# Batch 0's rows 96 to 111 by hardware queues, late table parts on GpSimd, batch 2's casts over more units

## The chip, the cores and the metric

One core of one Trainium2 chip runs the kernel. The metric is the device time of one execution in microseconds (us); shorter is better. The engines are PE (matrix products; PEld is its weight loading), DVE (vector), ACT (scalar), POOL (GpSimd, "Pool" in the text) and SP, which here only issues DMAs.

## The reference

Eight batches of 3072 x 256 numbers go through a two-dimensional Fourier transform, of which the real part is kept; the result goes through a feed-forward layer with three weight matrices and an elementwise maximum.

```
X = np.fft.fft(np.fft.fft(x, axis=1), axis=2).real          # x: (8, 3072, 256)
t = X.reshape(24576, 256)
h = np.maximum(np.maximum(t @ w1, t @ w2), t @ w3)          # (24576, 768)
out = h @ w_out                                             # (24576, 256)
```

## The kernel before

**Mixing.** The 3072 rows of a batch are split as 24 x 128 (`a`, `bb`), the 256 columns as 4 x 64 (`g`, `dl`). A batch lies in SBUF as 96 partitions (`g`, `a`) by 128 `bb` by 64 `dl`. In this text "rows 64 to 95" are values of `bb`; one transfer by `load_rows` brings 24 partitions of one `g`, so a range of rows takes four transfers. The real part needs each row together with its mirror image, so each batch is laid out twice as bfloat16: forwards (`lay_rows`, or the cast at L151) and reversed (`reverse`, `turn_rows`, or L154). Stage s (L492 with the forward layout, L494 with the reversed one, seven pieces) transforms over 24 and ends in `z_all`; stage k (L518, L520, six pieces `k(0)` to `k(5)`) transforms over 128 with a table `tab` of sines and ends in `t`. The transform over the columns is folded into the weights once (`prep_first`, L432, from `d2_bf`, `d3_bf` = w2 - w1, w3 - w1; `prep_second`, L451, L461).

**Feed-forward.** Each batch is worked through in 18 units (3 blocks of 512 columns by 6 slices of the hidden layer). A unit has products L538, L539 and L546, their maximum by ACT (L552) and DVE (L553), and a share of the previous block's output products (L563, L576, L587). For the output, DVE makes `other` (L590), Pool adds it to `even` (L593), DVE adds the sum to the products (`ot`, L613), half of which Pool scatters with an indirect DMA (L616, followed by a memset of `mark`) and half of which SP stores (L626). The output products have two PSUM banks; a bank is free again when its L613 is done.

**Order.** Nothing is scheduled: each engine runs its instructions in the order in which the program emits them. The list `plan` hangs pieces on units; they are emitted at the unit's end. Units are counted here from batch 0's first, so unit 24 is batch 1's seventh. Batch 1's stages s and k are spread over units 11 to 20, batch 2's begin at unit 24.

**Start.** Pool issues software transfers that cast to bfloat16 on the way: rows 0 to 95 in twelve transfers (32 rows each), rows 96 to 111 in four (16 rows each), then w1 (L214). SP and ACT bring rows 112 to 127 as float32 into `xs_a`, SP also the next group's first row (`load_next`, L115). SP then waits for one of the software transfers (`last_part[1]`, the fourteenth) and loads w2 and w3 (`raw_w`, L214), then batch 1 in four chunks of 32 rows (L103 by `load_chunk`, four buffers `xs`). DVE and ACT make the constants and the table and then the two layouts `nat` (by `lay_rows`, L365) and `back` (by `reverse` at L136) of batch 0. PE runs 31 warming products (L709) before the first real one. Pool waits with a memset (L410) for the last of DVE's copies (`laid`), then makes the row numbers (`store_rows`), the second halves of `d2_bf` and `d3_bf` (L186) and issues the load of w_out.

**Table.** `tab` has 13 rows of 128 angles, in three parts: sine, cosine, minus sine. `tab_angles` (L270, L274) makes angles, `tab_sines` (L281 to L285, ACT) the first two parts, `tab_minus` (L289) the third. Rows 0 to 6 are made at the start; rows 7 to 9 and 10 to 12 are "late": their angles by DVE at the start, parts of their sines by ACT in units 0, 2 and 3, their third part by Pool in units 1 and 3, each after a chunk of batch 1's casts. `k(3)` (unit 4) needs rows 7 and 8, `k(4)` (unit 6) rows 9 and 10.

**Batch 2's casts.** Pool casts and reverses all later batches. For batch 2 it does 16 half-chunk pieces (`turn_chunk(2, ch, part)`; parts 0 and 1 are L151, parts 2 and 3 L154), two a unit in units 14 to 21. Later batches have one a unit.

Of the kernel before, what the change touches and what calls it, by code (L numbers as in the profile page):

```python
# [9 lines left out]
FP32 = mybir.dt.float32  # L10
# [23 lines left out]
def kernel(  # L34
# [51 lines left out]
    half_pi = consts.tile([128, 64], FP32, tag="half_pi")  # L86
    w_late = consts.tile([128, 6 * 128], FP32, tag="w_late")
    twice = consts.tile([128, 256], FP32, tag="twice")
    sgn = consts.tile([128, 1], FP32, tag="sgn")
# [8 lines left out]
    def load_rows(engs, dst, b, r0, r1, after=None):  # L98
        lds = []
        xr = x_rows(b)  # L100
        for g in range(4):
            eng = engs[g] if isinstance(engs, tuple) else engs
            ld = eng.dma_start(out=dst[g * 24:(g + 1) * 24], in_=xr[g, :, r0:r1, :])  # L103
            if after is not None:
                tc.add_manual_dep(ld.ins, after.ins.name, AFTER, reason="weights first")
            lds.append(ld)
        return lds
# [92 lines left out]
    xs_a = xs_pool.tile([96, 33 * 64], FP32, name="xs", tag="xs")  # L200
    rows_a = xs_a[:, 0:17 * 64].rearrange("p (bb dl) -> p bb dl", dl=64)
    load_rows((nc.sync, nc.sync, nc.scalar, nc.scalar), rows_a[:, 0:16, :], 0, 112, 128)
    load_next(nc.sync, rows_a[:, 16:17, :], 0)

# [4 lines left out]
    for r0 in (0, 32, 64):  # L209
        load_rows(nc.gpsimd, x0v[:, r0:r0 + 32, :], 0, r0, r0 + 32)  # L210
    last_part = load_rows(nc.gpsimd, x0v[:, 96:112, :], 0, 96, 112)

# [7 lines left out]
    for jh in range(2):  # L220
        for wsrc, wdst in zip((moe_w2, moe_w3), raw_w):
            ld = load_w(nc.sync, wdst, wsrc, jh)
            if jh == 0:
                tc.add_manual_dep(ld.ins, last_part[1].ins.name, AFTER, reason="x first")

# [24 lines left out]
    nc.vector.tensor_scalar(out=p128, in0=pidx, scalar1=1.0 / 128.0, scalar2=None, op0=ALU.mult)  # L250
    pi13 = gen.tile([128, 13], FP32, tag="pi13")
    nc.vector.tensor_scalar(out=pi13, in0=j128[:, 0:13], scalar1=pidx, scalar2=1.0 / 3072.0,
                            op0=ALU.mult, op1=ALU.mult)

    step = gen.tile([128, 128], FP32, tag="step")
    near = gen.tile([128, 128], FP32, tag="near")
# [9 lines left out]

    def tab_angles(r0, r1):
        wr = rows_of(r0, r1)
        n = r1 - r0
        nc.vector.tensor_tensor(  # L270
            out=wr.rearrange("p (r j) -> p r j", j=128),
            in0=pi13[:, r0:r1].unsqueeze(2).to_broadcast([128, n, 128]),
            in1=step.unsqueeze(1).to_broadcast([128, n, 128]), op=ALU.subtract)
        nc.vector.scalar_tensor_tensor(out=wr, in0=wr, scalar=0.5, in1=wr,  # L274
                                       op0=ALU.is_gt, op1=ALU.subtract)

# [87 lines left out]
    def lay_rows(copy, xs, r0, n, d0=0, d1=33):  # L364
        return copy(  # L365
            out=xn0[:, d0:d1, r0:r0 + n],
            in_=bass.AP(xs.tensor, xs.offset + d0, [xs.ap[0], [1, d1 - d0], [64, n]]))

    def bf_rows(r0, n):
        return x0_first[:, r0 * 64:(r0 + n) * 64]  # L370

    on_act, on_dve = nc.scalar.copy, nc.vector.tensor_copy
    lay_rows(on_act, xs_a, 112, 16)
    reverse(on_dve, xr0, xs_a, 112, 17)
    on_dve(out=xr0[:, 32, 17:18], in_=xs_a[:, 0:1])
    turn_rows(on_act, 0, 31, 32, 65)
    tab_angles(7, 10)
    tab_angles(10, 13)
    vm = gen.tile([128, 256], FP32, tag="vm")
    qm = gen.tile([128, 256], FP32, tag="qm")  # L380
    nc.vector.tensor_scalar(out=vm[:, 0:128], in0=dvec, scalar1=pidx, scalar2=64.0,
                            op0=ALU.mult, op1=ALU.add)
    lay_rows(on_act, bf_rows(0, 32), 0, 32)
    tab_sines(7, 10, (0, 1))
    turn_rows(on_dve, 31, 32, 32, 65)
    lay_rows(on_dve, bf_rows(32, 32), 32, 32)
    nc.vector.tensor_scalar(out=vm[:, 128:256], in0=dvec, scalar1=pidx, scalar2=None,
# [5 lines left out]
                                   op0=ALU.add, op1=ALU.subtract)  # L393

    nc.scalar.activation(out=md[0], in_=vm, func=AX.Sin, scale=float(-2.0 * math.pi / 256.0))
    for (copy, a, b, c, d) in ((on_act, 54, 65, 20, 33), (on_dve, 32, 54, 0, 20)):
        turn_rows(copy, 63, 32, a, b)
        lay_rows(copy, bf_rows(64, 32), 64, 32, c, d)
    for (copy, a, b, c, d) in ((on_act, 58, 64, 22, 33), (on_dve, 32, 58, 0, 22)):
        turn_rows(copy, 95, 17, a, b)  # L400
        if copy is on_act:
            turn_rows(copy, 95, 16, 64, 65)
        laid = lay_rows(copy, bf_rows(96, 16), 96, 16, c, d)
    nc.vector.tensor_scalar(out=sgn, in0=pidx, scalar1=0.0, scalar2=None, op0=ALU.is_equal)
# [3 lines left out]
    for ch in range(4):  # L408
# [6 lines left out]
    nc.gpsimd.memset(gw[0:1, 512:513], 1.0)  # L415
    store_rows()
    differences(nc.gpsimd, 1)
    nc.gpsimd.dma_start(out=wout_bf.rearrange("p (jc c) -> p jc c", jc=NJC),
                        in_=moe_w_out.rearrange("(jc p) c -> p jc c", jc=NJC))

    def wide(t, cs):
# [362 lines left out]
    for (u, fn) in ((0, prep_some), (0, prep_some), (0, lambda: tab_sines(7, 10, (2,))),  # L784
                    (1, prep_some), (1, prep_some), (1, prep_some),
                    (2, lambda: m.k(2)), (2, prep_some), (2, lambda: tab_sines(10, 13, (0,))),
                    (3, prep_some), (3, lambda: tab_sines(10, 13, (1, 2))),
                    (4, lambda: m.k(3)), (4, prep_some), (5, prep_some), (5, l2_first),
                    (6, lambda: m.k(4)), (7, lambda: m.k(5)), (7, m.end),
                    (0, lambda: turn_chunk(1, 0)), (1, lambda: tab_minus(7, 10, nc.gpsimd)),  # L790
                    (2, lambda: turn_chunk(1, 1)), (3, lambda: tab_minus(10, 13, nc.gpsimd)),
                    (5, lambda: turn_chunk(1, 2)),
                    (7, lambda: turn_last(0)), (8, lambda: turn_last(1)),
                    (8, lambda: lay_last(0)), (9, lambda: lay_last(1)), (20, signed)):
        at(0, u, fn)
    for ch in range(4):
        at(0, (6, 7, 9, 11)[ch], lambda ch=ch: fetch(2, ch))
    for b in range(B - 1):
        for i, whats in enumerate(ahead):
            for what in whats:  # L800
                at(b, begin[b] + i if b else first_ahead[i], lambda b=b, what=what: piece(b + 1, what))
        if b + 2 < B:
            for ch in range(4):
                for part in range(4):
                    at(b, 6 + 4 * ch + part if b else 14 + 2 * ch + part // 2,
                       lambda b=b, ch=ch, part=part: turn_chunk(b + 2, ch, part))
                if b + 3 < B:
                    at(b, UNITS + (0, 1, 2, 4)[ch], lambda b=b, ch=ch: fetch(b + 3, ch))

# [78 lines left out]
```

## Time and profile before

| | us |
|---|---|
| median of 3 runs | 416.05 |
| lowest, highest | 415.71, 417.94 |
| the profiled execution | 416.61 |
| its span in the profile | 414.8 |
| PE busy | 394.1 (95%) |
| DVE busy | 309.2 (75%) |
| ACT busy | 266.9 (64%) |
| POOL busy | 318.2 (77%) |

The span runs from the first to the last instruction that the profile shows; 1.8 us of the execution lie around it. All rows of the profile are of this one execution, whose granted PE clock was 1.0. A row of the timeline gives start, duration, engine, line, operation, output and inputs, shapes and, in brackets, the idle time of the engine before it with what ended it. "xN" at its end means that N instructions in a row are merged. DMA issues appear on the issuing engine (SPq, ACTq, POOL); the duration is that of the issue, not of the transfer.

### The profile page before, as it was taken

How to read it: one execution, taken by the hardware profiler on the slowest of the kernel's cores; microseconds unless marked ns; L12 is line 12 of the kernel's file. 1: busy time of each engine (PE TensorE's matmuls, PEld its weight loads, DVE VectorE, ACT ScalarE, POOL GpSimd, SP SyncE). 2: the span in 40 equal slices, each digit the busy share in tenths (PEclk: the TensorE clock that was granted, in tenths of full speed). 3: DMA queues.
4: the chain of work that ended last, by engine and by line, in shares of the span. 5: the costliest groups of instructions: out<-in, count | busy, mean ns of one | idle time of the engine just before them, and what ended most of it. 6: DMA issues, size and time to landing. Idle time of an engine off the chain costs nothing.

```text
span 414.8 us, 9054 instructions
## 1 busy us (share of the span) xinstructions
PE 394.1 (95%) x3018; PEld 268.4 (65%) x3072; DVE 309.2 (75%) x559; ACT 266.9 (64%) x491; POOL 318.2 (77%) x429
## 2 busy tenths in 40 slices
PE   0988899989999999999999999999999999999996
PEld 0455667756676677667666666666676677766665
DVE  8887676776777777787668767687678777778884
ACT  7877667656765666756775666666676666655550
POOL 9846977999998888888878788888878844545651
PEclk9999999999999999999999999999999999999999
DMA  9998896574317852398216843287412222111314
GB/s 113 141 217 161 173 224 164 154 192 108 123 67 186 195 140 74 96 216 168 97 64 162 205 107 110 88 206 171 133 52 76 66 66 76 66 65 46 110 64 141
DMA packets 131175, 52.70 MB, mean 127 GB/s; under 512 B 113073, under 2 KB 128184, under 8 KB 131128
## 3 DMA queue, kind: packets, MB, share of 16 engines
q1 hardware_dynamic: 106496, 37.50, 36.6%
q0 software_dynamic: 23696, 14.29, 15.5%
q8 instruction: 24, 0.39, 0.4%
q10 hardware_dynamic: 936, 0.33, 0.3%
q14 instruction: 23, 0.19, 0.2%
HBM read 29.02 MB, written 25.17 MB: 131 GB/s over the span
## 4 chain that ended last, share of the span: by engine, by line
PE 86%; SPq 5%; POOL 4%; DMA 2%; issue 1%; DVE 0%; POOLq 0%
PE po L563 29%; PE pse L538 15%; PE pse L546 14%; PE pse L539 12%; SPq L103 4%; POOL x L103 3%; PE po L587 3%; PE ps L518 2%; PE ps L494 2%; PE ps L520 2%; PE ps L492 2%; PE pl L576 2%; DMA xs<-in_x_dram 1%; DMA x<-in_x_dram 1%; SPq L214 1%
## 5 line engine op out<-in xcount | busy, mean ns | idle before, releaser
L552 ACT ACTIVATE stmp<-pse 128x512 bf16<-128x512 f32 x288 | 171.2, 600 | 45.1 <-PE pse L539 26.7
L553 DVE TENSOR_TENSOR hp<-pse,stmp 128x512 bf16<-128x512 f32 x144 | 99.5, 691 | 89.4 <-ACT stmp L552 59.1
L616 POOL DMA_INDIRECT out_dram<-ot,rows_m x92 | 102.5, 1114 | 53.8 <-DVE ot L613 40.8
L538 PE MATMUL pse<-t,gE 128*128 128x512 bf16 x288 | 109.3, 379 | 2.1
L553 DVE TENSOR_TENSOR hm<-pse,stmp 128x512 bf16<-128x512 f32 x144 | 99.1, 689 | 3.7 <-ACT stmp L552 3.5
L539 PE MATMUL pse<-t,gO 128*128 128x512 bf16 x249 | 94.3, 379 | 0.0
L563 PE MATMUL po<-wout_bf,hp 128*128 128x256 bf16 x576 | 85.9, 273 | 0.0
L563 PE MATMUL po<-wout_bf,hm 128*128 128x256 bf16 x570 | 85.3, 273 | 0.1
L593 POOL TENSOR_TENSOR even<-even,other 128x256 f32<-128x256 f32 x92 | 66.5, 723 | 22.7 <-DVE other L590 20.4
L546 PE MATMUL pse<-t,gD 128*128 128x512 bf16 x273 | 82.4, 379 | 0.7
L563 PEld LDWEIGHTS <-hp 128*128 128x128 bf16 x576 | 56.2, 98 | 18.0 <-issue 2.8
L563 PEld LDWEIGHTS <-hm 128*128 128x128 bf16 x576 | 56.3, 98 | 16.6
L613 DVE TENSOR_TENSOR ot<-po,even 128x512 f32<-128x512 f32 x92 | 62.7, 682 | 0.7 <-POOL even L593 0.7
L151 POOL CAST x<-xs 96x544 bf16<-96x544 f32 (+2 forms) x51 | 58.7, 1155 | 4.6 <-DMA xs<-in_x_dram 4.6
L154 POOL CAST x<-xs 96x544 bf16<-96x544 f32 (+5 forms) x57 | 60.5, 1070 | 0.0
L522 ACT CAST t<-ps 128x512 bf16<-128x512 f32 x48 | 27.9, 585 | 36.5 <-PE ps L520 35.3
L546 PEld LDWEIGHTS <-gD 128*128 128x128 bf16 x288 | 27.9, 98 | 32.2
L499 ACT CAST z_all<-ps 128x480 bf16<-128x480 f32 x46 | 25.4, 559 | 35.2 <-PE ps L494 34.2
L590 DVE SCALAR_TENSOR_TENSOR other<-twice,po 128x256 f32<-128x256 f32 x92 | 43.8, 476 | 0.1
L539 PEld LDWEIGHTS <-gO 128*128 128x128 bf16 x288 | 28.1, 98 | 20.0 <-issue 1.8
L538 PEld LDWEIGHTS <-gE 128*128 128x128 bf16 x288 | 28.1, 98 | 19.9 <-issue 0.7
L579 ACT COPY even<-pl 128x512 f32<-128x512 f32 x46 | 27.0, 587 | 9.6 <-PE pl L576 9.2
(168 smaller groups left out, 382.9 us busy)
## 6 DMA issues: line engine op xcount, KB each, us to landing
xs<-in_x_dram SPq DMA_DIRECT2D x84, 198.0 KB
out_dram<-ot SPq DMA_DIRECT2D x90, 128.0 KB
xs<-in_x_dram SPq DMA_DIRECT2D x28, 192.0 KB
raw_w<-in_moe_w_dram SPq DMA_DIRECT2D x4, 384.0 KB
out_dram<-ot,rows_m POOLq DMA_INDIRECT x92, 3.8
x<-in_x_dram POOLq DMA_DIRECT2D x12, 96.0 KB, 5.3
out_dram<-ot SPq DMA_DIRECT2D x17, 64.0 KB
xs<-in_x_dram SPq DMA_DIRECT2D x32, 5.8 KB
```

The costliest lines, as they stand in the source:

```text
L151: nc.gpsimd.tensor_copy(v[:, d0:d1, ch * 32:ch * 32 + 32], xs[:, 0:32 * 64].rearrange("p (bb dl) -> p dl bb", dl=64)[:, d0:d1, :])
L154: reverse(lambda out, in_: nc.gpsimd.tensor_copy(out, in_), v[:, 33:66, :], xs, ch * 32, 33 if ch == 3 else 32, 32 + d0, 32 + d1)
L538: nc.tensor.matmul(pse[:, 0:n], gE[i][:, js], te, start=True, stop=False)
L539: nc.tensor.matmul(pse[:, 0:n], gO[i][:, js], to, start=False, stop=True)
L546: nc.tensor.matmul(pse, gD[i][:, js], to, start=False, stop=True, skip_group_check=True)
L552: nc.scalar.activation(out=stmp[:, 0:n], in_=pses[0][:, 0:n], func=AX.Relu)
L553: nc.vector.tensor_tensor(out=dst, in0=src3, in1=stmp[:, 0:n], op=ALU.max)
L563: nc.tensor.matmul(po, hcols(jc), wout_bf[:, jc * 256:(jc + 1) * 256], start=False, stop=(jc == NJC - 1), skip_group_check=True)
L590: nc.vector.scalar_tensor_tensor(out=other, in0=twice, scalar=po[:, 256:257], in1=po[:, 0:256], op0=ALU.mult, op1=ALU.subtract)
L593: nc.gpsimd.tensor_tensor(out=line[:, 256:512], in0=line[:, 0:256], in1=other, op=ALU.add)
L613: nc.vector.tensor_tensor(out=ot, in0=po, in1=lin, op=ALU.add)
L616: stored(nc.gpsimd.indirect_dma_start(out, bass.IndirectOffsetOnAxis(ap=rows_m[0:128 - lo, b * 12 + slot: b * 12 + slot + 1], axis=0), ot[ ...
```

## The change

Rows 96 to 111 of batch 0 no longer come by four software transfers: SP loads them as float32 into `xs_a` with four transfers behind its first ones. Pool issues twelve transfers of 32 rows, and `raw_w` waits for the ninth of them (the first of rows 64 to 95). DVE and ACT share the layouts anew: the 32 rows 96 to 127 come from `xs_a`; DVE lays rows 0 to 31 out forwards, the two engines share rows 32 to 63, and the last step, shared too, is rows 64 to 95.

Of the late table, the angles of rows 10 to 12 are made by Pool after the issue of w_out's load, in three operations in place of DVE's two; the third part of rows 7 to 9 is made by Pool before the differences, that of rows 10 to 12 in unit 2 ahead of chunk 1's casts.

Batch 2's sixteen half-chunk casts are hung on units 11 to 23, at most two on a unit: 11 11 12 13 14 15 15 16 17 18 19 19 20 21 22 23. The fetch of batch 3's last chunk moves by two units. On PE the order of instructions stays the same.

```diff
     xs_a = xs_pool.tile([96, 33 * 64], FP32, name="xs", tag="xs")
-    rows_a = xs_a[:, 0:17 * 64].rearrange("p (bb dl) -> p bb dl", dl=64)
-    load_rows((nc.sync, nc.sync, nc.scalar, nc.scalar), rows_a[:, 0:16, :], 0, 112, 128)
-    load_next(nc.sync, rows_a[:, 16:17, :], 0)
+    rows_a = xs_a.rearrange("p (bb dl) -> p bb dl", dl=64)
+    load_rows((nc.sync, nc.sync, nc.scalar, nc.scalar), rows_a[:, 16:32, :], 0, 112, 128)
+    load_next(nc.sync, rows_a[:, 32:33, :], 0)
+    load_rows(nc.sync, rows_a[:, 0:16, :], 0, 96, 112)
...
     for r0 in (0, 32, 64):
-        load_rows(nc.gpsimd, x0v[:, r0:r0 + 32, :], 0, r0, r0 + 32)
-    last_part = load_rows(nc.gpsimd, x0v[:, 96:112, :], 0, 96, 112)
+        last_part = load_rows(nc.gpsimd, x0v[:, r0:r0 + 32, :], 0, r0, r0 + 32)
...
             if jh == 0:
-                tc.add_manual_dep(ld.ins, last_part[1].ins.name, AFTER, reason="x first")
+                tc.add_manual_dep(ld.ins, last_part[0].ins.name, AFTER, reason="x first")
...
-    def tab_angles(r0, r1):
+    def tab_angles(r0, r1, eng=nc.vector):
...
+        if eng is nc.vector:
...
+        else:
+            eng.tensor_scalar(out=w_high[:, 0:n * 128], in0=wr, scalar1=0.5, scalar2=None,
+                              op0=ALU.is_gt)
+            eng.tensor_tensor(out=wr, in0=w_high[:, 0:n * 128], in1=wr, op=ALU.subtract)
...
-    lay_rows(on_act, xs_a, 112, 16)
-    reverse(on_dve, xr0, xs_a, 112, 17)
-    on_dve(out=xr0[:, 32, 17:18], in_=xs_a[:, 0:1])
+    lay_rows(on_act, xs_a, 96, 32)
+    reverse(on_dve, xr0, xs_a, 96, 33)
+    on_dve(out=xr0[:, 32, 33:34], in_=xs_a[:, 0:1])
     turn_rows(on_act, 0, 31, 32, 65)
+    lay_rows(on_dve, bf_rows(0, 32), 0, 32)
     tab_angles(7, 10)
-    tab_angles(10, 13)
...
-    lay_rows(on_act, bf_rows(0, 32), 0, 32)
     tab_sines(7, 10, (0, 1))
     turn_rows(on_dve, 31, 32, 32, 65)
-    lay_rows(on_dve, bf_rows(32, 32), 32, 32)
...
+    lay_rows(on_act, bf_rows(32, 32), 32, 32, 17, 33)
     nc.scalar.activation(out=md[0], in_=vm, func=AX.Sin, scale=float(-2.0 * math.pi / 256.0))
-    for (copy, a, b, c, d) in ((on_act, 54, 65, 20, 33), (on_dve, 32, 54, 0, 20)):
-        turn_rows(copy, 63, 32, a, b)
-        lay_rows(copy, bf_rows(64, 32), 64, 32, c, d)
-    for (copy, a, b, c, d) in ((on_act, 58, 64, 22, 33), (on_dve, 32, 58, 0, 22)):
-        turn_rows(copy, 95, 17, a, b)
+    lay_rows(on_dve, bf_rows(32, 32), 32, 32, 0, 17)
+    for (copy, a, b, c, d) in ((on_act, 55, 64, 21, 33), (on_dve, 32, 55, 0, 21)):
+        turn_rows(copy, 63, 33, a, b)
         if copy is on_act:
-            turn_rows(copy, 95, 16, 64, 65)
-        laid = lay_rows(copy, bf_rows(96, 16), 96, 16, c, d)
+            turn_rows(copy, 63, 32, 64, 65)
+        laid = lay_rows(copy, bf_rows(64, 32), 64, 32, c, d)
...
     store_rows()
+    tab_minus(7, 10, nc.gpsimd)
     differences(nc.gpsimd, 1)
     nc.gpsimd.dma_start(out=wout_bf.rearrange("p (jc c) -> p jc c", jc=NJC),
                         in_=moe_w_out.rearrange("(jc p) c -> p jc c", jc=NJC))
+    tab_angles(10, 13, nc.gpsimd)
...
-                    (0, lambda: turn_chunk(1, 0)), (1, lambda: tab_minus(7, 10, nc.gpsimd)),
-                    (2, lambda: turn_chunk(1, 1)), (3, lambda: tab_minus(10, 13, nc.gpsimd)),
+                    (0, lambda: turn_chunk(1, 0)), (2, lambda: tab_minus(10, 13, nc.gpsimd)),
+                    (2, lambda: turn_chunk(1, 1)),
...
-                    at(b, 6 + 4 * ch + part if b else 14 + 2 * ch + part // 2,
+                    at(b, 6 + 4 * ch + part if b else 11 + 13 * (4 * ch + part) // 16,
...
-                    at(b, UNITS + (0, 1, 2, 4)[ch], lambda b=b, ch=ch: fetch(b + 3, ch))
+                    at(b, UNITS + (0, 1, 2, 4 if b else 6)[ch], lambda b=b, ch=ch: fetch(b + 3, ch))
```

More of the change, by code (lines that the diff above doesn't have):

```diff
@@ L87 @@
     w_late = consts.tile([128, 6 * 128], FP32, tag="w_late")
+    pi_all = consts.tile([128, 64], FP32, tag="pi_all")
+    pi13 = pi_all[:, 0:13]
+    step = consts.tile([128, 128], FP32, tag="step")
+    w_high = consts.tile([128, 3 * 128], FP32, tag="w_high")
     twice = consts.tile([128, 256], FP32, tag="twice")
@@ L250 @@
     nc.vector.tensor_scalar(out=p128, in0=pidx, scalar1=1.0 / 128.0, scalar2=None, op0=ALU.mult)
-    pi13 = gen.tile([128, 13], FP32, tag="pi13")
     nc.vector.tensor_scalar(out=pi13, in0=j128[:, 0:13], scalar1=pidx, scalar2=1.0 / 3072.0,
                             op0=ALU.mult, op1=ALU.mult)
-    step = gen.tile([128, 128], FP32, tag="step")
     near = gen.tile([128, 128], FP32, tag="near")
@@ L265, in rows_of @@
         return (w_late if r0 >= 7 else w)[:, (r0 % 7) * 128:(r0 % 7 + r1 - r0) * 128]
-    def tab_angles(r0, r1):
+    def tab_angles(r0, r1, eng=nc.vector):
         wr = rows_of(r0, r1)
         n = r1 - r0
-        nc.vector.tensor_tensor(
+        eng.tensor_tensor(
             out=wr.rearrange("p (r j) -> p r j", j=128),
@@ L273, in tab_angles @@
             in1=step.unsqueeze(1).to_broadcast([128, n, 128]), op=ALU.subtract)
-        nc.vector.scalar_tensor_tensor(out=wr, in0=wr, scalar=0.5, in1=wr,
-                                       op0=ALU.is_gt, op1=ALU.subtract)
+        if eng is nc.vector:
+            eng.scalar_tensor_tensor(out=wr, in0=wr, scalar=0.5, in1=wr,
+                                     op0=ALU.is_gt, op1=ALU.subtract)
+        else:
+            eng.tensor_scalar(out=w_high[:, 0:n * 128], in0=wr, scalar1=0.5, scalar2=None,
+                              op0=ALU.is_gt)
+            eng.tensor_tensor(out=wr, in0=w_high[:, 0:n * 128], in1=wr, op=ALU.subtract)
     def tab_sines(r0, r1, parts=(0, 1, 2)):
```

## The prediction

> **What bounds the kernel now.** All times are us from the start of the profiled execution; line numbers are those of the kernel before. First the page: PE is busy 95% of the span, and the chain of work that ended last puts nearly all of it on PE.
>
> ```profile
> PE 86%; SPq 5%; POOL 4%; DMA 2%; issue 1%; DVE 0%; POOLq 0%
> ```
>
> So only PE's idle time can be won or lost. I looked for it in PE's own timeline, keeping the rows with idle time before them.
>
> ```profile
> 18.55 0.20 PE L492 MATMUL ps<-m24f,nat 96*128 96x96 bf16 x1 [0.80 <-DVE sgn L404]
> ...
> 22.09 0.82 PE L432 MATMUL psg<-d_bf,md_all 128*128 128x384 bf16 x4 [0.64 <-DVE d_bf L186]
> ...
> 25.95 0.81 PE L432 MATMUL psg<-d_bf,md_all 128*128 128x384 bf16 x4 [0.37 <-POOL d_bf L186]
> ...
> 35.67 0.27 PE L518 MATMUL ps<-tab,z_all 128*128 128x256 bf16 x1 [0.77 <-POOL tab L289]
> ...
> 43.87 0.27 PE L518 MATMUL ps<-tab,z_all 128*128 128x256 bf16 x1 [1.31 <-POOL tab L289]
> ...
> 91.74 0.27 PE L587 MATMUL po<-gw,t 128*128 128x257 bf16 x1 [0.94 <-DVE ot L613]
> ```
>
> These six are where the change can act; after 100 us the table of 10 us stretches has PE busy 9.89 to 9.95 of 10 up to 410. Next, what feeds the first rows: Pool's timeline, a piece of the chain of waits, and the stretch from 5 to 10 us (busy time and count of PE, PEld, DVE, ACT, POOL; then clock, DMA share, GB/s).
>
> ```profile
> 1.47 13.91 POOL L103 DMA_DIRECT2D x<-in_x_dram  x16 [0.29 <-issue]
> 15.37 1.77 POOL L214 DMA_DIRECT2D w_bf<-in_moe_w_dram  x2
> ...
> 12.53 3.49 DMA x<-in_x_dram
> ...
> 5.00:10.00 5.00, 0.55 (x2) 0.29 (x3) 4.43 (x30) 4.39 (x12) 5.00 (x7) 1.00 2.07 123
> ```
>
> Pool issues 16 software transfers of batch 0's rows until 15.37. The 14th, issued at 12.53, lands at 16.02 and lets SP start raw_w. DVE and ACT then lay the rows out:
>
> ```profile
> 9.23 0.99 DVE L136 CAST back<-xs 96x544 bf16<-96x544 f32 x2
> ...
> 12.26 1.10 DVE L136 COPY back<-x 96x1056 bf16<-96x1056 bf16 x1
> ...
> 17.50 0.53 DVE L136 COPY back<-x 96x442 bf16<-96x442 bf16 x1 [0.58 <-DMA x<-in_x_dram]
> ...
> 9.14 1.10 ACT L365 CAST nat<-xs 96x528 bf16<-96x528 f32 x1
> ```
>
> Both engines work almost without a break from 9.2; DVE waits only 0.58 for the last rows. So the start is set nearly as much by this copying as by the transfers. Last, Pool around the stall at 91.74:
>
> ```profile
> 90.25 0.72 POOL L593 TENSOR_TENSOR even<-even,other 128x256 f32<-128x256 f32 x1
> 90.92 2.32 POOL L154 CAST x<-xs 96x561 bf16<-96x561 f32 x3
> 93.39 0.98 POOL L616 DMA_INDIRECT out_dram<-ot,rows_m  x1 [0.16 <-DVE other L590]
> ```
>
> This L593 had its operand since DVE's L590 at 85.13, five us earlier: two casts a unit in units 14 to 21 have put Pool behind.
>
> **Part 1, rows 96 to 111 by SP.** Pool loses transfers 13 to 16, 15.37 - 11.83 = 3.5 us, though each is half size (0.7 to 1.0 us, against 0.82 to 0.87 for most full ones). SP gains four issues behind its nine, at about 4.5 to 6.2 (0.4 each, by its rows at 0.74 and 1.23); nothing queued behind them was ready, since raw_w waited until 16.02 anyway. When do these rows land? They are 4 x 24 x 16 = 1536 rows. SP's and ACT's first four transfers move as many, issued from 0.74 to 2.0, and their packets end at about 4.5: some 3.8 from the first issue, so 8.3 with nothing beside them. Beside the software stream, whose 10752 rows take about 11.6 us by the packet records (930 a us), they may get half the turns: 1536 / 465 = 3.3 us. With 1.45 from issue to first packet (raw_w: 16.04 to 17.5) and 0.45 from last packet to use (17.0 to 17.46) that is 4.5 + 5.2 = 9.7. I take 10.0. The software rows are held up by 0 (engines not full) to 1536 / 930 = 1.65 us (full); I take 0.7.
>
> The Trainium skill, "DMA: Bandwidth & Descriptors", section "Issuing engines are not separate DMA queues", says that transfers from all issuers share the same 16 engines, so that another issuer saves only issue time. That rule would mean the full 1.65 us, rival B below.
>
> **The copies of the first rows.** The new order on DVE, from the steps of before (start to start): reversing 33 rows in place of 17 from xs, 1.2 in place of 0.67; lay_rows of rows 0 to 31, 1.0; one pair of tab_angles, 1.05 (the other, 1.05, has gone to Pool); vm 0.25; reverse 32 rows 1.0; vm to L392 1.2; half a lay_rows 0.55: 6.3 in all, then 0.75 + 0.75 for rows 64 to 95. ACT: lay 32 rows from xs 2.0 in place of 1.0, reverse 1.9, sines 1.1, half a lay 1.0, md 0.35, then 0.6 + 0.2 + 0.85: 8.0. From 10.0 DVE ends at 17.8 and ACT at 18.0; from 9.15, as before, ACT ends at 17.15, but PE's 31 warming products last until 17.76 in any case. Rows 64 to 95 were in by 15.51 (DVE reversed them then without a wait), so with 0.7 more by 16.2, when both engines get to them. PE starts at about 18.2 in place of 18.55: **0.35 won**, between -0.9 (rows seen at 11.2) and 0.75.
>
> **raw_w, then everything behind it.** SP now waits for the ninth transfer. It was issued at 8.18 and took 5.2 to land: 13.4 in place of 16.02. With the hold-up above the shift is 2.6 down to 1.0; I take 1.9. w1 moves 3.5 earlier on Pool. Then the waits of 0.64 (DVE's raw_w) and 0.37 (Pool's) go, even with PE 0.35 early.
>
> **Part 2, the table on Pool.** tab_minus(7,10), 1.18, now runs at about 19.5 before the differences, where Pool waited 3.59 for raw_w: free, and the 0.77 at 35.67 goes. tab_minus(10,13) moves ahead of chunk 1's casts: it ends near 35.5, the products that waited at 43.87 come near 40, so 1.31 goes. tab_angles(10,13) is new work on Pool, three operations of 128x384: tensor_tensor 128x256 took 0.72 and 128x768 1.65, so about 0.95 twice, and 1.18 for the comparison (L289's): 3.1 after the wout issue, ending near 30.3 (26.37 + 1.65 + 0.92 - 1.9 + 3.1). ACT's sine of these rows ran at 31.63 and wants it near 30.2: 0 to 0.8 of a wait, taken as 0.1. Chunk 0's casts wait for it too, but were waiting for their transfer (to 30.34 - 1.9 = 28.4) and are not what is late next.
>
> What is late next is wout: its products at 36.25 waited for its transfer, whose issue shifts with raw_w, by 1.9. So PE's gain there is the smaller of 0.35 + 0.64 + 0.37 + 0.77 = 2.1 and 1.9. With 1.31 it is **3.2** at unit 6. Batch 1's chunks also land 1.9 earlier, and Pool saves a tab_minus between them (1.18), so its casts, which before ended 0.4 ahead of PE's first use at 56.2, end 3.1 earlier: no new stall.
>
> **Part 3, batch 2's casts over units 11 to 23.** In old time, Pool's idle 2.8 and 1.4 us at 60.5 to 65.8 now take four half-chunk casts, and with one cast in most units the sum (casts 1.1, L593 0.7, L616 with its memset 1.25) keeps up: the L593 that came at 90.25 comes near 86.5, and the stall of 0.94 is gone but for 0.2 or so. But the last cast now stands behind unit 23's L616, which waits for that unit's ot. DVE's L590 there is at 89.80, ot ends at 90.97 at best, L616 runs to 92.15, and the cast (1.2 by L173's two) to 93.45. Adding up Pool's work from 59.8 on, cast by cast, gives 93.8. PE's first reversed product of batch 2 was at 93.11 before, both stalls included; now 93.5 to 93.85. **0.7 lost** (0.3 to 0.9): the stall moves and grows.
>
> The rest costs nothing: pi, step and the scratch tile move to another pool without an instruction, and batch 3's last chunk is fetched two units later, 12 units (over 30 us) ahead of its first cast, on an SP queue that waits for stores there anyway.
>
> **Sum.** 3.2 - 0.7 = 2.5 on the profiled execution, 416.61 (414.8 of span and 1.8 around it): 414.1. The median of the runs is 416.05, 0.56 lower: 413.5.
>
> **Rivals.** *A, all of the gain*: the engines have room, x and raw_w come as early as the rows of before allow (2.6), PE starts at 17.8, the last cast costs 0.3: 0.75 + 0.64 + 0.37 + 0.77 = 2.5, with 1.31 and less 0.3 it is 3.5: 412.5. For it: the DMA share falls with Pool's smaller transfers, so Pool set the pace. *B, the transfers share full engines*: raw_w shifts by 1.0 and PE's start by nothing: 1.0 + 1.31 - 0.8 = 1.5, 414.5. For it: a share of 2.07 that hardly varies at 4 to 11 us. *C, raw_w overtakes x (slower)*: before, two half transfers were open behind the one that releases raw_w, and x was in (17.0) when raw_w's first packets came (17.5); now three full ones, 2304 rows, are open. If many are still open 1.45 us after the release, each turns with a raw_w packet; raw_w's 1.57 MB take 5.5 us at the 283 GB/s of 19 to 20 us. All of that on x (15.4 to 20.9) starts PE at 22.6, 4.05 late; the four removed waits (3.1) and the cast's 0.7 stay: -4.05 + 3.1 - 0.7 = -1.65, 417.7; half of it gives 415. It decides from 3.9 us of delay on; against it, the ninth lands late (5.2), when most later rows have moved. "DMA: Bandwidth & Descriptors" of the Trainium skill, section "Queues, rings and completion order", has each engine take turns between its queues by packets, which is how C would work. *D, no effect at the start*: the copies take longer than I add up and only the Pool table's 1.31 and the casts count: 416.05 - 0.6.
>
> **How the numbers follow.** Forecast 0.51 (its own range 412.8 to 414.4), A 0.14, B 0.15, C 0.12, D 0.04, and 0.04 for a loss that no row of before shows. A measurement of this kernel tells about 0.5%, 2.1 us, from no change, so faster is under 414.0: 0.44 of the forecast and all of A, 0.58. Slower, over 418.1, needs C at its worst with a longer cast stall (0.04) or the unseen loss (0.04): 0.08. The same: 0.34. Range 411.8 to 416.9: it leaves out C's upper end, the unseen loss and a little of A, under 0.2.
>
> **What would show it.** Right: 12 software issues ending near 11.9, raw_w issued at 14 to 15, PE's first L492 near 18.2, no idle before the L518 of 35.67 and 43.87, and a PE wait of 1.4 to 1.8 on Pool's last L154 of batch 2 (near 91) in place of L587's 0.94. Wrong: ACT or DVE idle at 9.2 for over 2 us; x rows landing after 17; a new wait of ACT for w_late; PE waiting for batch 1's casts near 53.

## The result, and the profile after

The changed kernel takes 422.34 us (median of 4 runs, 422.22 to 423.02); the kernel before, run beside it, 415.88. The ratio is 1.0154, interval 1.0111 to 1.0198: slower, and outside the range that was forecast. The profiled execution took 422.26 with a span of 420.5, which is 5.7 longer than before. Line numbers from here on are those of the changed kernel (3 to 7 more than before), unless a version of the kernel before is named.

The page first: the busy line of PE, and the chain that ended last.

```profile
PE 398.1 (95%) x3018; PEld 271.2 (64%) x3072; DVE 308.7 (73%) x556; ACT 266.3 (63%) x489; POOL 318.7 (76%) x428
...
PE 91%; POOL 2%; DVE 2%; issue 2%; DMA 1%; ACT 0%; DVEq 0%; POOLq 0%; ACTq 0%
```

PE does the same instructions, yet is busy 4.0 longer (394.1 before): part of the loss is not waiting at all. In the first 100 us, behind the warming products, PE's timeline has two waits left of over half a microsecond:

```profile
21.39 0.20 PE L497 MATMUL ps<-m24f,nat 96*128 96x96 bf16 x1 [2.28 <-DVE sgn L407]
...
96.61 0.22 PE L499 MATMUL ps<-m24r,x 96*128 96x96 bf16 x1 [3.36 <-POOL x L158]
```

All six rows that the prediction showed are gone or replaced: the waits for `d_bf`, for the two negated table parts and for the bank (L587 before) are away, as forecast. (For the two of the table this is not shown to be the table's doing: in e_rows below, where the table is made as before and PE also comes late, they are gone too.) In their place stand a start 2.84 later (21.39 against 18.55) and a wait of 3.36 for Pool's last cast of batch 2. What feeds the start, in the timeline of ACT, DVE, Pool and SP:

```profile
13.30 2.01 ACT L372 CAST nat<-xs 96x1056 bf16<-96x1056 f32 x1 [4.05 <-DMA xs<-in_x_dram]
...
13.60 1.20 DVE L140 CAST back<-xs 96x1056 bf16<-96x1056 f32 x2 [4.27 <-DMA xs<-in_x_dram]
...
1.47 10.01 POOL L107 DMA_DIRECT2D x<-in_x_dram  x12 [0.29 <-issue]
12.11 0.75 POOL L218 DMA_DIRECT2D w_bf<-in_moe_w_dram  x1 [0.62 <-DMA x<-in_x_dram]
...
15.60 0.42 SPq L218 DMA_DIRECT2D raw_w<-in_moe_w_dram  x1
```

Pool's issues do end early (11.5 instead of 15.4). But rows 96 to 111, on SP's queue since 4.93, are read only at 13.3; ACT and DVE, which the prediction wanted to feed at 10.0, stand idle for over 4 us; and `raw_w` goes out 0.44 earlier than before, not 1.9.

Then the clock. These are stretches around both waits (busy time and count of PE, PEld, DVE, ACT, POOL; granted PE clock; DMA share; GB/s):

```profile
22.00:25.00 3.00, 3.00 (x42) 3.00 (x39) 2.30 (x5) 1.12 (x2) 2.60 (x6) 0.50 0.92 169
...
94.00:97.00 3.00, 0.39 (x9) 0.39 (x10) 0.00 (x0) 0.00 (x0) 3.00 (x5) 1.00 0.14 27
97.00:101.00 4.00, 4.00 (x20) 2.05 (x18) 1.74 (x3) 1.97 (x4) 1.44 (x2) 0.57 0.45 97
```

After each of the two waits PE works at half its clock for 3.41 us, by the clock records of the trace from 21.96 to 25.38 and from 97.06 to 100.47. Half of 3.41, twice, is 3.4 of the 4.0 us of extra busy time. Last, Pool around the second wait:

```profile
90.69 1.18 POOL L158 CAST x<-xs 96x561 bf16<-96x561 f32 x1
91.82 0.72 POOL L598 TENSOR_TENSOR even<-even,other 128x256 f32<-128x256 f32 x1
92.90 2.59 POOL L621 DMA_INDIRECT out_dram<-ot,rows_m  x1 [0.36 <-DVE hp L558]
...
95.52 1.20 POOL L158 CAST x<-xs 96x495 bf16<-96x495 f32 x2
```

The last cast stands behind a scatter that took 2.59. The prediction gave it 1.0, what the others take.

As a ledger: batch 1's first product comes at 57.25 against 56.22 before (+1.0; 3.2 earlier was forecast), the second group of ten of batch 2's first products at 100.97 against 95.78 (+5.2 in all), the end +5.7. The last 0.5 was not taken apart.

### The profile page after: what moved, and what is told of

It reads as the page before. It is cut to its first block, busy times and chain, and to the rows that moved or that the text cites. A ratio compares the mean times of both kernels' runs of the same rounds, so it can differ in the third digit from the quotient of the medians.

```text
span 420.5 us, 9047 instructions
## 1 busy us (share of the span) xinstructions
PE 398.1 (95%) x3018; PEld 271.2 (64%) x3072; DVE 308.7 (73%) x556; ACT 266.3 (63%) x489; POOL 318.7 (76%) x428
## 4 chain that ended last, share of the span: by engine, by line
PE 91%; POOL 2%; DVE 2%; issue 2%; DMA 1%; ACT 0%; DVEq 0%; POOLq 0%; ACTq 0%
PE po L568 30%; PE pse L543 16%; PE pse L551 15%; PE pse L544 13%; PE ps L497 3%; PE ps L499 3%; PE po L592 3%; PE ps L523 3%; PE ps L525 3%; PE pl L581 2%; POOL x L107 2%; DMA x<-in_x_dram 1%; DVE nat L372 1%; DVE hm L558 0%; DVE back L140 0%
```

## The experiments

Theory 1: rows 96 to 111 come late because their packets share the same transfer engines with Pool's software stream. Theory 2: batch 2's stall is the last cast behind the batch's last scatter. Theory 3, formed on seeing the first results: a wait of PE is paid twice, since the clock halves after it. "Before" is each time the median of the kernel before on the same chip. It lay between 414.9 and 416.1, so where a version is called nearer than the changed kernel, its distance from "before" is set against the changed kernel's 6.5.

### The parts alone

**e_rows**: the kernel before with the change at the start only (the first hunks of the diff; `raw_w` behind the ninth transfer).

> Only the rows part (rows 96 to 111 by SP, raw_w behind the ninth transfer, the layouts shared anew); table and casts as before. Theory 1 (the start was lost to the hardware rows, which get a third of the turns beside the software stream): ACT and DVE wait some 4 us at 9.2, the rows are seen at 13.3, PE's first product is at 21.4, its clock then drops for 3 to 4 us, and stage k begins near 26.6, 3.9 later than before. The table waits of 0.77 and 1.31 shrink or vanish, since Pool's casts of batch 1 are no later than before and PE is; at unit 6 some 1.6 remain and nothing gives them back: slower than before by 1.0 to 2.5. Rival (all of 5.7 us was lost at the start and only shows later): slower by 4 or more.

420.82, before 415.37, ratio 1.014 (1.0092 to 1.0188); four runs from 418.74 to 423.0, the profiled one being the lowest. `xs` is read at 13.4 and 13.7, PE starts at 22.50 after 4.32 idle, and 23 to 27 us pass at a clock of 0.50 to 0.76. DVE still makes the angles of rows 10 to 12 here (1.05), which the expected 21.4 left out. Part 1 alone loses 5.4 by the medians, where theory 1 had said 1.0 to 2.5 and its rival 4 or more: the size went to the rival. The profiled execution lost 2.2 of span; why two of the four took 422 to 423 is not shown.

**e_table**: the kernel before with the table's part only.

> Only the table part (angles of rows 10 to 12 by Pool, both third parts earlier on Pool). Theory (as forecast): PE's idle 0.77 and 1.31 go, the first is partly taken by the wait for w_out, so faster by 1.3 to 2.1; the waits at the start (0.80, 0.64, 0.37) and the stall of 0.94 at 91.7 stay. Rival (DVE loses 1.05 of work at the start and Pool gains 3.1): if DVE sets the start, PE also starts up to 0.5 earlier, 2.5; if Pool's 3.1 hold up chunk 0's casts or ACT's sine, no gain.

414.88, ratio 0.9988 (0.9971 to 1.0006): not clear of no change, where 1.3 to 2.1 were expected. The 0.77 and the 1.31 are gone, but there are new waits on PE and, for the late angles, on ACT; the last three lines are Pool's:

```profile
28.58 0.81 PE L440 MATMUL psg<-d_bf,md_all 128*128 128x384 bf16 x4 [0.54 <-POOL d_bf L190]
34.19 0.38 PE L546 MATMUL pse<-t,gE 128*128 128x512 bf16 x1 [0.41 <-ACT stmp L560]
...
32.64 0.52 ACT L288 ACTIVATE tab<-w_late 128x384 bf16<-128x384 f32 x1 [0.46 <-POOL w_late L282]
...
20.84 1.19 POOL L296 TENSOR_SCALAR tab<-tab 128x384 bf16<-128x384 bf16 x1
24.24 1.64 POOL L190 TENSOR_TENSOR d_bf<-raw_w,w_bf 128x768 bf16<-128x768 f32 x1 [2.22 <-DMA raw_w<-in_moe_w_dram]
26.89 1.64 POOL L190 TENSOR_TENSOR d_bf<-raw_w,w_bf 128x768 bf16<-128x768 f32 x1 [1.00 <-DMA raw_w<-in_moe_w_dram]
```

The negation (L296) holds nothing up here: behind it Pool still waits 2.22 and then 1.00 for `raw_w`, and the 0.54 on PE comes from that second wait. e_best2 below, which has no negation at this place, shows the same two waits (0.97 on Pool, 0.51 on PE). ACT's sine does wait for Pool's angles. Up to batch 1's first product 1.4 was won.

**e_casts**: the kernel before with batch 2's casts over units 11 to 23 only.

> Only the casts part (batch 2's casts over units 11 to 23). Theory 2 (the last cast stands behind the scatter of the batch's last slot, which takes 2.6 and not 1.0): that scatter takes 2.6, PE waits 3 to 3.5 at the first reversed product of batch 2, its clock drops for some 4 us behind that wait, and with the 0.94 and 0.28 of before gone the kernel is slower by 3.5 to 4.5. Rival (the forecast's size: scatter 1.0, wait 1.8, no drop of the clock): slower by 0.3 to 0.9.

420.55, ratio 1.0095 (1.0065 to 1.0124); the six times lie in two groups, 418.1 and 418.2, and 420.5 to 420.9. By the medians that is 5.2 slower, more than the 3.5 to 4.5 expected. The scatter and the wait are as theory 2 has them, and its rival falls:

```profile
91.71 2.58 POOL L616 DMA_INDIRECT out_dram<-ot,rows_m  x1 [0.20 <-DVE hp L553]
...
95.41 0.22 PE L494 MATMUL ps<-m24r,x 96*128 96x96 bf16 x1 [3.19 <-POOL x L154]
```

The three parts alone don't add up to the whole: 5.4 - 0.5 + 5.2 is 10.1, against 6.5 for the changed kernel. Where the difference lies was not taken apart.

### The scatter

**e_scatter112**: the changed kernel, with the scatter of each batch's last slot shortened from 127 rows (from partition 1 on) to 112 (from partition 16 on). It leaves 15 rows of every batch but the last unwritten.

```diff
-  ap=rows_m[0:128 - lo, ...], ot[lo:128, 256:512]
+  ap=rows_m[0:128 - 16 * lo, ...], ot[16 * lo:128, 256:512]
```

> The changed kernel, but the scatter of each batch's last slot moves 112 rows instead of 127 (the 15 rows left out are not written in any batch but the last). Theory 2a (127 rows are what makes it slow, since they don't divide over the engines): it takes about 1.0, PE's wait for the last cast falls from 3.4 to about 1.8 and its clock stays up, so faster than the changed kernel by 1.6 to 3.6: 418.7 to 420.7. Rival (it is slow because of its place, at a batch's end, or because it waits for its queue): it stays at 2.6 and the time stays at 422.3.

418.07, ratio 1.0064 (1.0039 to 1.0089): 2.7 over the kernel before, so 3.8 nearer than the changed kernel.

```profile
90.39 0.97 POOL L621 DMA_INDIRECT out_dram<-ot,rows_m  x1 [0.17 <-DVE hp L558]
```

With 112 rows the scatter takes 0.97 like one with 128; with 127 it takes 2.59. Whether the number of rows or the first partition does it stays open, since this version changes both. PE's wait fell to 1.54 and no half clock followed. Its ten times fall in two groups, and the mean granted clock of each run sorts them: five runs at 416.15 to 417.14 have 1.000, five at 419.01 to 419.78 have 0.991 to 0.994. The profiled one is of the first: PE started at 20.64 after 2.60 idle, at full clock. So the same program runs with a half clock in some executions and without it in others, which makes a difference of about 2.6; at which place it came in the other five is not seen, since they have no trace.

**e_after22**: the changed kernel with the sixteen casts over units 11 to 22, so that none follows the batch's last scatter; all the work is done.

```diff
-  11 + 13 * (4 * ch + part) // 16
+  11 + 12 * (4 * ch + part) // 16
```

> The changed kernel with batch 2's casts over units 11 to 22 instead of 11 to 23, so that no cast stands behind the batch's last scatter of 2.59; all the work is done, and the late start is still in. Theory (that scatter is the whole of the loss at batch 2): PE idle under 0.5 at batch 2's first product, no half clock there, time 416.0 to 418.3, as in the run with scatters of 112 rows (418.07). Rival (the casts of the last units come late in any order): over 1.5 idle there, time over 420.

417.16, ratio 1.0036 (1.0005 to 1.0067): 2.0 over the kernel before, so 4.5 nearer than the changed kernel, and PE has no wait of note at batch 2. This is most of the loss, removed by one number. Four of its runs have a clock of 0.992 to 0.996; the fifth, at 1.000, took 414.49.

### The start

**e_warm38**: the changed kernel with 38 warming products (`range(31)` becomes `range(38)`).

> The changed kernel with 38 warming products instead of 31, so that they last about 2.2 us longer (0.31 each), to some 21.3, and PE has next to no idle time ahead of its first transposing product at 21.39 (2.28 in the changed kernel). Theory: the half clock in 22 to 25 comes from that idle time and not from the transposing products; then the granted clock stays at 1.0 in 20 to 28, the last step of the start (stage k) comes at 24.3 to 25.0 instead of 26.63, batch 1's first product 1 to 2.3 earlier than 57.25, and the time falls by 1 to 2.3, to 420 to 421.3. Rival: the clock falls whatever PE did before, since the products themselves or the transfers draw it down: clock 0.5 again, time within 0.5 of 422.3.

420.24, ratio 1.0121 (1.0087 to 1.0155). The changed kernel's is 1.0154, and the two intervals overlap, so what tells here is the trace. PE starts almost when it did, with less idle time ahead; the second line is the stretch after it, with the clock ahead of the last two numbers.

```profile
21.29 0.20 PE L497 MATMUL ps<-m24f,nat 96*128 96x96 bf16 x1 [1.06 <-DVE sgn L407]
...
22.00:25.00 3.00, 2.97 (x59) 2.38 (x55) 2.66 (x6) 2.36 (x7) 2.60 (x6) 1.00 0.86 143
```

59 products instead of 42 in the same 3 us: theory 3 holds for the start, and batch 1's first product came 1.7 earlier (55.59).

**e_early**: the changed kernel with rows 96 to 111 issued ahead of the next row (`load_rows` moved above `load_next`).

> The changed kernel with the four transfers of rows 96 to 111 ahead of SP's five small ones of the next row, so 2.3 earlier in SP's queue; nothing else. Theory 1 (those transfers lose turns to the software stream that begins to move at 4.0, and get some 360 packets of 256 B per us beside it instead of 410 on this queue alone): rows seen at 10.5 to 11.5 instead of 13.3, PE's first transposing product at 18.9 to 19.7 instead of 21.39, so idle under 0.8 and no half clock at the start; batch 1's first product 54.5 to 55.5; time 419.0 to 420.5, with batch 2's late cast still in. Rival (the queue is in order and its 3168 packets take as long however they are ordered, to 13): rows seen at 12.8 to 13.4, time within 0.7 of 422.3.

420.3, ratio 1.0116 (1.0081 to 1.0151). Half right: ACT reads its rows at 10.35, but DVE's reversal also needs the next row, which is now behind them and is seen at 12.74. PE started at 20.70, a microsecond later than expected, after 1.79 idle, and the half clock came again.

**e_spread**: the same, and two of the four transfers by ACT.

```diff
-    load_rows(nc.sync, rows_a[:, 0:16, :], 0, 96, 112)
+    load_rows((nc.sync, nc.sync, nc.scalar, nc.scalar), rows_a[:, 0:16, :], 0, 96, 112)
```

> As the kernel before it in this list (rows 96 to 111 ahead of the next row), and two of the four transfers issued by ACT, whose queue moved 440 packets per us beside SP's 410 in 3 to 4 us; ACT pays 0.97 for the two issues. Theory 1a (each hardware queue has turns of its own): rows seen by 8.5 to 9.9, where ACT and DVE become free, PE's first transposing product at 17.5 to 18.5, no half clock at the start, batch 1's first product 53.0 to 54.5, time 417.5 to 419.5 with batch 2's late cast still in. Rival 1b (the two hardware queues share one third of the turns beside the software stream): rows seen at 10.5 to 11.5, as with one queue, time 419.0 to 420.5.

420.2, ratio 1.0119 (1.0082 to 1.0156).

```profile
9.17 1.96 ACT L372 CAST nat<-xs 96x1056 bf16<-96x1056 f32 x1
...
12.43 1.30 DVE L140 CAST back<-xs 96x1056 bf16<-96x1056 f32 x2 [3.10 <-DMA xs<-in_x_dram]
```

The rows themselves were in time, so theory 1a's arrival was right, but not its 417.5 to 419.5: the next row was late, and PE started at 20.27. Its idle time was 1.63, with no half clock at the start; batch 1 began at 54.75. The next row's last packet moved at 10.66, 1.8 before DVE read it; in the changed kernel that distance is 0.5 (12.80 to 13.30). What fills the rest is not shown.

**e_spread2**: the split between the queues, with the next row back ahead of SP's half.

> The changed kernel with rows 96 to 111 issued half by SP (still behind its five small transfers of the next row) and half by ACT; nothing else. With the rows ahead of the next row, DVE waited for the next row instead (12.43); this order leaves the next row where it was. Theory (two queues, and 768 packets on SP's in place of 1536): both reads of the rows at 9.2 to 10.3, PE's first transposing product at 17.5 to 18.6, no half clock at the start, batch 1's first product 52.5 to 54.5; time 417.5 to 419.3, with batch 2's late cast still in. Rival (the start is held by the software rows and the copies behind them, not by rows 96 to 111): reads at 9.2 to 10.3 but the first transposing product at 19.5 to 20.5, time 419.8 to 420.6.

420.47, ratio 1.0133 (1.0105 to 1.016). A miss: 12.62 for ACT, 12.91 for DVE. SP's 768 packets still had to pass beside the software stream, and ACT's first sine began 2.4 later (5.88 instead of 3.44). In these versions whatever was put last on the queues was read at 12.4 to 13.7.

**e_ready**: rows ahead of the next row and on two queues, DVE's angles and its copy of rows 0 to 31 moved ahead of the reversal into the gap, 29 warming products, casts to unit 22.

> The changed kernel with rows 96 to 111 ahead of the next row and half on ACT's queue (rows at 9.2 for ACT, next row at 12.4 for DVE, as that version showed), DVE doing the table's angles (1.1) and the copy of rows 0 to 31 (1.1) in the gap of 3.1 ahead of its reversal, 29 warming products, and batch 2's casts to unit 22. Theory (the start follows the copies, and these the arrival): PE's first transposing product at 17.8 to 18.8 instead of 20.27 there, batch 1's first product 52.3 to 53.5, no half clock; time 411.0 to 412.8, under every version so far (413.55). Rival (what the shorter stream brings is lost in the waits for the experts' weights behind it): first transposing product at 17.8 to 18.8, but batch 1's first product at 54.0 or later, time 413.3 to 415.

415.48, ratio 0.9987 (0.9969 to 1.0005): no gain, though the waits for `xs` are gone. Neither side was right, since PE started at 19.91. What is late next are the software rows:

```profile
15.54 1.09 ACT L372 COPY nat<-x 96x512 bf16<-96x512 bf16 x1 [0.40 <-DMA x<-in_x_dram]
...
15.57 1.09 DVE L140 COPY back<-x 96x1056 bf16<-96x1056 bf16 x1 [0.79 <-DMA x<-in_x_dram]
```

Both read rows between 31 and 63. In the kernel before DVE began to reverse them at 12.26 and to lay them out at 13.28, without a wait. What the hardware rows gain in time, the software rows lose. (PE's idle time was 2.35, and the half clock came here too.)

**e_norows** tests that. It is e_after22 without the hardware transfers of rows 96 to 111: DVE fills their place with zeros, and the 12 software transfers stay.

> The changed kernel with batch 2's casts to unit 22, and with rows 96 to 111 of batch 0 not loaded at all: DVE fills their place with zeros (some 1.1, behind its table), so the output lacks these rows; the 12 software transfers stay. Theory (the hardware packets took their turns from the software stream): x's 9216 software packets end at 15.0 to 15.6 instead of 16.99 (the kernel before moved 10752 of them in the 13.2 from 3.9 to 17.16, so 11.4 for 9216), PE's first transposing product at 17.3 to 18.6, time 412.5 to 415. Rival (the software stream has a pace of its own, set by Pool's issues or its ring): its packets end at 16.5 to 17.0 again, PE's first transposing product at 18.6 or later, time over 415.

412.34, ratio 0.9923 (0.9902 to 0.9945).

```profile
18.26 0.20 PE L497 MATMUL ps<-m24f,nat 96*128 96x96 bf16 x1 [0.45 <-DVE sgn L407]
...
12.78 2.52 SPq L217 DMA_DIRECT2D raw_w<-in_moe_w_dram  x4
```

Batch 1's first product comes at 52.56. From the packet records of the trace, in us (software packets of 128 B, one for a row of 64 numbers; hardware packets of 256 B):

| kernel | software: count, first, half, last | hardware: count, last |
|---|---|---|
| before | 10752, 3.84, 9.88, 17.08 | 1632, 8.40 |
| changed | 9216, 3.86, 10.96, 16.95 | 3168, 12.80 |
| e_spread | 9216, 4.93, 10.51, 16.39 | 3168, 10.66 |
| e_norows | 9216, 3.96, 9.16, 14.88 | 1632, 8.21 |

Taking 1536 software packets away ends the stream 2.2 earlier (17.08 to 14.88). Putting the same rows back as hardware packets costs 2.1 of that (16.95); over the five traces with the changed kernel's transfers the stream ends between 16.50 and 17.14, so it is 1.6 to 2.3. Theory 1 is shown, and more than that: the rows of x take their turns whichever queue they come by, so the change had next to nothing to win in the arrival of x. Even without these rows PE starts only 0.29 earlier than in the kernel before (18.26 against 18.55); what e_norows wins lies behind that, with `raw_w` issued 3.26 earlier (12.78 against 16.04).

### Versions meant to be faster

**e_casts22**: the kernel before with the casts over units 11 to 22 alone.

> The kernel before with batch 2's casts spread over units 11 to 22 alone. Theory: the stall of 0.9 in unit 23 of batch 0 goes and nothing comes in its place; time 0.3 to 1.0 under the kernel before. Rival (the faster times of the version with the moved table parts came from those alone): within 0.3 of the kernel before, or over it.

414.57, before 415.15, ratio 0.9975 (0.9958 to 0.9993), and the wait of 0.94 is gone: as forecast.

**e_best2**: the same, and the two negations moved, with all angles left on DVE.

```diff
+    tab_minus(7, 10, nc.gpsimd)          # behind the issue of w_out's load
...
-    (0, lambda: turn_chunk(1, 0)), (1, lambda: tab_minus(7, 10, nc.gpsimd)),
-    (2, lambda: turn_chunk(1, 1)), (3, lambda: tab_minus(10, 13, nc.gpsimd)),
+    (0, lambda: turn_chunk(1, 0)), (2, lambda: tab_minus(10, 13, nc.gpsimd)),
+    (2, lambda: turn_chunk(1, 1)),
```

> The kernel before, with two things alone: both negated table parts leave their old place (the first goes on Pool behind the output weights' issue, the second ahead of the second turning of batch 1), the angles stay on DVE; and batch 2's casts are spread over units 11 to 22, so that the last one follows a scatter of 128 rows and not the batch's last one of 127 rows, which takes 2.59. Theory: the waits of 0.77 and 1.31 for the negated parts go, the new waits of the version with angles on Pool (0.54, 0.41, 0.24) don't come, the last cast is done by 93 and PE waits less than 0.3 at batch 2's first product, and the stall of 0.9 in unit 23 of batch 0 goes; time 412.5 to 414.2 against 415.4. Rival: the last cast is still ahead of the batch's last scatter or behind it at PE's need (over 1.5 idle and a lower clock again): 417 to 420.

413.55, before 414.9, ratio 0.9963 (0.9945 to 0.9981), 12 runs from 412.95 to 415.1. Pool around the same place as above, in the lines of this version:

```profile
88.00 1.23 POOL L154 CAST x<-xs 96x495 bf16<-96x495 f32 x2
...
90.12 2.58 POOL L617 DMA_INDIRECT out_dram<-ot,rows_m  x1 [0.20 <-issue]
```

The scatter is as long as ever, but the last cast is ahead of it, and PE has no wait there. Two waits for `d_bf` behind Pool, of 0.52 and 0.51, came all the same. Batch 1 begins at 54.25, 1.7 earlier than in e_casts22 (55.99). Of the versions that do all the work this is the fastest, though its interval overlaps that of e_casts22.

**e_best4**: the changed kernel with its three parts corrected (the queues of e_spread2, casts to unit 22, the first negation behind the angles).

> The changed kernel with three corrections: rows 96 to 111 half on ACT's queue; casts to unit 22; and the first negated table part behind the late angles on Pool, so behind the differences, not ahead of them. Theory: PE's first transposing product at 17.5 to 18.6, no half clock at the start or at batch 2, waits for d_bf under 0.6 in all; time 411.5 to 413.3, under the version of the kernel before with moved casts and table parts (413.55). Rival (the shorter stream of x brings nothing that the end sees): 413.3 to 414.5.

415.6, ratio 1.0008 (0.9995 to 1.002). A miss for the theory: PE started at 20.95 behind reads at 12.85 and 13.14. The clock was 1.0 and batch 1's first product came at 56.18, as before the change: with the start as it is, the rest only makes up for it.

## Why the prediction was wrong

The sum had 413.5 and the chip gave 422.34. Taking the profiled executions (414.1 forecast, 422.26 measured), the sum misses 4.2 up to batch 1's first product (53.0 forecast, 57.25 measured), 3.5 at batch 2 (0.7 lost forecast, 4.2 measured) and 0.5 behind it.

- **"Rows 96 to 111 ... I take 10.0."** The failed step of Part 1. The rows were assumed to move at half the turns, 465 a us, in 3.3 us. In the changed kernel's packet records their first packet moves at 6.83, 1.9 after the issue and right behind the next row's last one (6.81) on the same queue, whose 96 packets take from 3.92 on; and their last at 12.80: 6.0 us, 257 a us. The view of the DMA queues of the changed kernel, from 7 to 11 us (packets, MB, share of 16 engines), has the hardware packets at 31% of the turns, 305 a us:

```profile
q0 software_dynamic: 2693, 0.28, 115.9%
q1 hardware_dynamic: 1219, 0.30, 47.3%
```

  So they are read at 13.3, beyond the bound of 11.2. From there on the sum was right: 8.1 from the read to PE's start (13.30 to 21.39), where the copies had been added up to 8.0 on ACT. Two readings of the kernel before were off as well: x's software packets take 13.2 us from first to last (3.84 to 17.08), 812 a us and not 930, and SP has seven issues ahead of the new ones, not nine.
- **"The software rows are held up ... I take 0.7."** They were held up by 2.1 (16.95 against 14.88; 1.6 to 2.3 over the five traces), over the upper end of 1.65. So `raw_w` shifted by 0.44 and not 1.9; without the hardware rows it shifted by 3.26. Here lies the root: Pool's issue time (3.5) was taken as what the stream costs, while the transfer engines set its pace. Pool's twelve issues end at 11.5 in the changed kernel and at 11.9 in e_norows, yet the stream ends at 16.95 and 14.88. The Trainium skill's page "DMA: Bandwidth & Descriptors", section "Issuing engines are not separate DMA queues", says that another issuer saves the issue time alone. The trace agrees, with 2.1 of 2.2 us given back. Rival B held this mechanism, but let PE start when it did before, at the price of 1.0.
- **The clock: a term that the sum lacked.** In the kernel before no wait behind the warming products was followed by a lower clock; the longest was 1.31. Here PE's idle time ahead of its first real product, by run: 0.33, 0.41, 0.45, 0.57, 0.59, 0.80, 1.06 and 1.63 gave no half clock, 1.79, 2.28, 2.35, 4.07 and 4.32 did, and 2.60 did not in its profiled run. At batch 2, waits of 3.19 to 3.37 did, 1.54 did not. The clock records of the traces order these. Within an execution the clock changes only at whole steps of 3.41 us, which lie elsewhere in each execution, and a stretch at half clock lasts one step or two. In the step just before each fall PE was idle for 1.79 to 2.99 of the 3.41; steps at full clock with less than 1.79 idle were followed by another at full clock, and so was one of e_rows with 1.92. The 2.60 was divided between two steps, 1.78 and 0.83, while the 1.79 of e_early lay in one. The page "TensorE: Matmul & The Clock Gate" of the Trainium skill, Part 1, has the clock fall to half after an idle window of some 3.4 us that runs freely. The traces agree in the length and the free phase, but the window need not be idle as a whole: 1.79 was enough here. Of the 4.2 missed up to batch 1, one step at half clock is up to 1.7 (3.41 x 0.5); the start is 3.2 later than forecast (21.39 against 18.2), and 0.7 came back in between.
- **Part 3, "L616 runs to 92.15".** The placing was right (the last cast behind unit 23's scatter, PE waiting for it), the size was not: 2.59 instead of 1.0. The row stood in the profile of before, at a place where nothing waited for it:

```profile
95.38 2.58 POOL L616 DMA_INDIRECT out_dram<-ot,rows_m  x1 [0.20 <-issue]
```

  1.6 of the 3.5 missed is this row. In the 3.41 us at half clock behind it PE lost up to another 1.7.
- **Part 2** was right in what goes (0.77, 1.31; e_table alone shows it, since e_rows loses both waits too, with the table as before) and in the price of the three angle operations (0.84 + 1.18 + 1.00 = 3.0, forecast 3.1). "Free" for the negation ahead of the differences held in e_table, where Pool waited for `raw_w` behind it. In the changed kernel Pool reaches it only at 23.59, it takes 1.97, and the differences follow without a wait, so there it was in the way, though PE shows no wait for it. The sine's wait, taken as 0.1, was 0.46 in e_table, whose gain is not clear of no change. The sum's end of the angles, "near 30.3", adds up to 30.1.
- **The stall at 91.74** went as forecast, and e_casts22 shows that it does so without a new one if the last cast keeps ahead of that scatter.
- **Rival C** did not occur: x's last software packet (16.95) is no later than before (17.08). The loss came by a path that the rivals had only as "a loss that no row of before shows", although two of its three parts could be read there: the scatter's row, and the full transfer engines. Of the signs of being wrong that the prediction named, the first came: ACT and DVE idle at 9.2 for over 4 us.

What stays open: what besides PE's idle time in a step decides the clock (1.78 in e_scatter112 and 1.92 in e_rows passed, 1.79 in e_early did not, and in e_ready and e_spread a second step at half clock followed); why the next row is read up to 1.8 after its last packet; and why the scatter of 127 rows takes 1.6 longer than one of 112 or 128.

## What to carry to other kernels

Before moving transfers to another queue, see whether the transfer engines or the issuing engine sets the pace: leave the transfers out in one run, and the time that they can give is known. When work is moved behind an instruction, take that very instruction's row and not the group's usual duration. And count a wait of PE of about 2 us or more twice, with the half clock that may follow it; a few more warming products can remove the second part.

## What was not expected of the hardware

- An indirect scatter of 127 rows, from partition 1 on, holds Pool for 2.56 to 2.60, most of those of 128 rows for 0.97 to 1.02, those of 112 rows for 0.94 to 0.97.
- PE's granted clock fell to 0.50 for 3.41 or 6.83 us when PE had been idle for 1.79 or more of the 3.41 us before. One program, whose executions had a half clock or not, took 2.6 of 418 longer with it.
- Two hardware queues moved 430 and 435 packets in one us before the software stream was under way (e_early, 3 to 4 us); beside it one queue moved 305 a us (changed kernel, 7 to 11 us).
